# First MoE layer: products with packed values times w_in in place of x times w_in, parts of w_in kept in DRAM

## The chip, the cores and the metric

The kernel runs on one core of one Trainium2 chip. The metric is device time in microseconds (us) of one execution. The kernel before takes 1510.52 us, the median of three executions (1508.63 to 1512.57).

## The reference, cut to what matters

```python
# attention through 32 packs for each head: batch 8, heads 8, sequence 576, head_dim 64
p_packed = sm_attn(p, k, v)              # 32 packed rows of 64 for a head
out = sm_attn(q, p_packed, p_packed)     # softmax(q . p_packed) gives shares of 32 packs; shares @ p_packed
x = out.transpose(0, 2, 1, 3).reshape(4608, 512)
# first MoE: one dense hidden layer of 2048
h = x @ w_in                             # 512 -> 2048
g = h * clip(h + 3, 0, 6) / 6
x1 = g @ w_out                           # 2048 -> 512
# second MoE: 8 experts, one for each token, 512 -> 1024 -> 512
```

For one batch element, x is (shares of 8 heads x 32 packs = 256 numbers for each token) times a block matrix of packed values. So x @ w_in is also shares @ (packed values @ w_in), a product over 256 and not over 512, once the second factor is known.

## The kernel before

Every fp32 operand is split into an upper and a lower part of TensorE's faster format, and each product is made of three matmuls (`mm3`: upper by upper, upper by lower, lower by upper). PE is TensorE, DVE is VectorE, ACT is ScalarE, POOL is GpSimd, SP issues most DMAs.

The 4608 tokens go through the first MoE in 16 blocks of 288, two blocks to a batch element. A block has 16 steps (`g` counts steps over all blocks, `fc` in a block). A step has the first layer of 128 hidden units (`m1_l1`, PE tile `hps`, two halves), its activation (ACT `r`, then the gate on DVE, `m1_gate`), its split (ACT `gh`, POOL `gl`, `m1_split`), and the second layer of the step two before it (`m1_l2`, PE tiles `acc`). In PSUM there are two tiles `hps`, two tiles `tps` that everything else shares, and four `acc`.

Between the halves stand ticks, four to a step. Each tick lets every running generator do its next piece once its wait (a number of ticks in `WT`) is over: `qstage` turns the next block's q into x (scores `s2`, softmax over packs on DVE, then products `al` by `pbh` and `pbl`, which make x and its parts `xh`, `xl`), `kstage` makes the packed values of a batch element and one half of its heads (`pph`, `ppl` are their turned parts), and `m1_end` writes a finished block to DRAM and routes its tokens. One `kstage` runs in each of blocks 0 to 13. Each engine executes its instructions in the order in which they are written.

At the start the float64 weights w_in and w_out come in 32 pieces of 512 KB. `w_stage` turns each to fp32 parts in five stages over ACT, DVE and POOL. A hand-written string `ORDER` says which chain steps next, also inside block 0, up to the last weight piece. In the last block the first slots of the second MoE are chosen and loaded (`pre_slots`), and 12 slots of 384 tokens then run through the experts.

Of the kernel before, what the change touches and what calls it, by code (L numbers as in the profile page):

```python
# [36 lines left out]
WT = {  # L37
    "p": 4, "k": 4, "exp": 7, "aT": 6, "pp": 9, "ppT": 6, "q": 7, "s2": 6, "sm": 7, "out": 5, "w": 4, "x1": 8, "lp": 3,
    "oh": 6, "sc": 4, "s0": 0, "sw": 7, "ga": 0, "tu": 3, "y": 4, "tb": 1, "s1": 0, "s2q": 17, "y0": 9, "mp": 5,
}  # L40
# [4 lines left out]
ORDER = "dddeedeaddeeadbdebaadeaadaededaawaebeaeabfbbaabwbbbabbaffbafbwwafwfawwbwbabwagbabawawwbaaaggawgbwwwbwaabawbawwwggwwwwwbabwwwwwbwgwbwawwbaawwbwkwbwbwcawbwwbwwww.wwbbbkqwqwqww.qkwqww.qwwkwk.kqwkqwk.qqkwkqwqkw.kqk.wkwwwqwwqwkw.qqk.qkkqqwwwwqw..wqkkqwwwwqkqkwq.wwkw.qkwwwwqqww.qkwkqqwwwwqk...wkwwwkwqwqwkww.w.ww.qwqqwwww.wwwww..q.wwww.w....ww.wwww.ww.ww..w...w.ww..www..w.w.wwwwww....ww..www.w..w...wwww.ww..."  # L45
W_MIN = 2.0 ** -15  # the upper word of a float64 of 2**-127, read as a float32
# [3 lines left out]
def kernel(ctx, tc, q, k, v, p, w_in, w_out, mod_id, w_gate, mod_bias, w1, w2, out):  # L50
# [7 lines left out]
    # left: weights, constants, x of even blocks, attention; the last two make room for the second MoE  # L58
    # right: tiles of hidden layers, x of odd blocks, first the raw weights and then the first MoE's results
# [16 lines left out]
    tabd = dp.tile([NTAB, 2], I32, name="tabd")  # L76

# [28 lines left out]
    pph, ppl, pbh, pbl = [], [], [], []  # L106
    for hq in range(2):
        pph.append(ap.tile([128, 2, 128], F32R, name=f"pph{hq}"))
        ppl.append(ap.tile([128, 2, 128], F32R, name=f"ppl{hq}"))
        pbh.append(ap.tile([128, 2, 128], F32R, name=f"pbh{hq}"))  # L110
        pbl.append(ap.tile([128, 128], F32R, name=f"pbl{hq}"))
# [19 lines left out]
    def late_consts():  # L131
        # what only the start needs lies where weights will lie
# [27 lines left out]
        # token of column tg*32+i of a block, on partition (tg%3, i)  # L160
# [12 lines left out]
        # entries that no token fills: no output row, a row of zeros, no gate  # L173
# [33 lines left out]
    script = []  # L207

    def tick():
        if script:  # L210
            if scripted():
                return
            streams[:0] = [s for s in script if not s.done]
            script.clear()
# [13 lines left out]
    class Feed:  # L228
        """Half sequences of four heads of q or k, in order: their rows, turned and split by halves of d."""

        def __init__(self, src, units, depth, pool=None):
            self.apart = True  # runs as a chain of its own, at the start
            self.src, self.units, self.depth, self.pool = src, units, depth, pool
            self.raw, self.n, self.ready = [], 0, []
# [14 lines left out]
        def ahead(self):  # L249
            """[(h, c), (sg, si)] of the next half of d, which is 32e + c."""  # L250
# [38 lines left out]
    # the first heads go in two chains at once; the second one's tiles lie where weights will lie  # L289
# [25 lines left out]
    def turned(hi, lo, src, f=None):  # L315
        """[(h, n), (h % 2, e, c)], zeros elsewhere, to blocks of [(h, c), e, (h, n)] in two parts."""
# [16 lines left out]
    # rows of a pair of heads, the other rows, the pair  # L333
    pairs = [(slice(0, 64), slice(64, 128), 0), (slice(64, 128), slice(0, 64), 1)]

    def kstage(b, hq):
        """Scores of the packs, their weights, the packed values and their transposes."""
# [63 lines left out]
        while b > 0 and ("q", b - 1, 1, hq) not in done:  # L401
            yield 1
# [16 lines left out]
        for r, _, j in pairs:  # L419
            nc.scalar.copy(pbh[hq][r, j, :], mb[r])  # L420
        yield
        for r, o, j in pairs:
            nc.gpsimd.tensor_tensor(pbl[hq][r], mb[r], r32(pbh[hq][r, j, :]), op=ALU.subtract)
            nc.scalar.copy(pbh[hq][o, j, :], mb[r])
        yield from turned(pph[hq], ppl[hq], mb, mf)
# [5 lines left out]
    def qstage(b, hf, hq):  # L431
# [51 lines left out]
        for r, _, j in pairs:  # L483
# [8 lines left out]
            if j == 0:  # L492
                yield WT["out"]
# [643 lines left out]
```

## Time and profile before

| | us |
|---|---|
| median of three executions | 1510.5 |
| span of the profiled execution, first to last instruction | 1508.5 |
| start, to the first product of block 1 | 169.5 |
| blocks 1 to 13, each about | 61.0 |
| block 14 (no `kstage`) | 56.4 |
| block 15, to the first product of the second MoE | 65.9 |
| second MoE, to the end of the span | 423.0 |

The profiled execution's own time is its span and about 2 us around it, as the median lies 2.0 us above the span. Engines are asynchronous, so busy times overlap. A matmul's row lasts longer than its share of the time, since matmuls are pipelined: what one costs is read from start to start.

### The profile page before, as it was taken

The numbers are of one execution on the slowest core, as the hardware profiler recorded it, in microseconds if no ns is written. First come the engines' busy times: TensorE is split into PE (matmuls) and PEld (weight loads), VectorE is DVE, ScalarE is ACT, GpSimd is POOL, SyncE is SP. The second block draws the span as 40 slices with busy tenths as digits, with TensorE's granted clock in tenths as the row PEclk, the third lists the DMA queues.
The fourth block names the chain that finished last, engine by engine and source line by source line (L and its number), as shares of the span: only waits on it lengthen the run. The fifth ranks groups of instructions, "written<-read, shape, count | busy, mean of one in ns | idle before, by whom it ended". The sixth has DMA issues, their size and how long they took to land. (4 is left out here: it accounts for less than half of the span.)

```text
span 1508.5 us, 25124 instructions
## 1 busy us (share of the span) xinstructions
PE 1412.0 (94%) x9072; PEld 1329.4 (88%) x9072; DVE 898.4 (60%) x2211; ACT 684.7 (45%) x1503; POOL 673.4 (45%) x774
## 2 busy tenths in 40 slices
PE   3367899999999999999999999999999999999995
PEld 2257899999999999999999999999889999999994
DVE  8999756464465554645646556446666656566541
ACT  6556545454354454544544535433434434444430
POOL 3678644444444444444444444433135544444530
PEclk8578999999999999999999999999899999999998
DMA  9333112011120111111201110003336555555520
GB/s 273 126 135 100 42 25 59 23 49 40 26 66 24 41 47 29 55 42 25 64 18 48 40 33 33 17 1 118 102 121 209 168 172 165 172 168 194 180 89 30
DMA packets 111301, 127.03 MB, mean 84 GB/s; under 512 B 52163, under 2 KB 77892, under 8 KB 111172
## 3 DMA queue, kind: packets, MB, share of 16 engines
q1 hardware_dynamic: 102148, 106.41, 22.7%
q0 software_dynamic: 9024, 18.96, 3.7%
q8 instruction: 73, 1.20, 0.3%
q14 instruction: 56, 0.46, 0.1%
HBM read 105.80 MB, written 19.54 MB: 83 GB/s over the span
## 5 line engine op out<-in xcount | busy, mean ns | idle before, releaser
L97 POOL TENSOR_TENSOR gl<-r,gh 128x288 fp32r<-128x288 f32 x240 | 199.1, 830 | 277.0 <-ACT gh L96 212.2
L91 PE MATMUL acc<-gh,wh 128*128 128x288 f32 x1024 | 311.8, 304 | 2.3 <-ACT gh L96 1.2
L92 PE MATMUL acc<-gl,wh 128*128 128x288 f32 x1024 | 305.1, 298 | 8.1 <-POOL gl L97 6.0
L91 PE MATMUL hps<-xh,wh 128*128 128x288 f32 x1024 | 309.5, 302 | 1.7 <-issue 1.3
L93 PE MATMUL hps<-xh,wl 128*128 128x288 f32 x1024 | 306.5, 299 | 1.9 <-POOL wl L561 1.5
L92 PE MATMUL hps<-xl,wh 128*128 128x288 f32 x1024 | 305.6, 298 | 1.9 <-DVE xl L490 1.8
L93 PE MATMUL acc<-gh,wl 128*128 128x288 f32 x1024 | 306.3, 299 | 0.8 <-issue 0.8
L596 DVE SCALAR_TENSOR_TENSOR r<-r,hps 128x288 f32<-128x288 f32 x256 | 114.1, 446 | 226.6 <-ACT r L591 226.1
L794 POOL DMA_INDIRECT xg<-x1d,idx x144 | 152.7, 1060 | 171.3 <-DVE idx L789 131.1
L92 PEld LDWEIGHTS acc<-gl,wh 128*128 128x128 f32 x1024 | 195.0, 190 | 9.6 <-POOL gl L97 7.3
L91 PEld LDWEIGHTS acc<-gh,wh 128*128 128x128 f32 x1024 | 194.9, 190 | 8.3 <-ACT gh L96 1.8
L91 PEld LDWEIGHTS hps<-xh,wh 128*128 128x128 f32 x1024 | 196.4, 192 | 5.5 <-issue 1.1
L92 PEld LDWEIGHTS hps<-xl,wh 128*128 128x128 f32 x1024 | 196.5, 192 | 3.0 <-DVE xl L490 2.2
L93 PEld LDWEIGHTS hps<-xh,wl 128*128 128x128 f32 x1024 | 196.2, 192 | 2.6 <-POOL wl L561 1.8
L93 PEld LDWEIGHTS acc<-gh,wl 128*128 128x128 f32 x1024 | 194.9, 190 | 2.7 <-issue 2.7
L591 ACT ACTIVATE r<-hps,half 128x288 f32<-128x288 f32 x256 | 127.5, 498 | 131.0 <-PE hps L93 121.1
L274 POOL TENSOR_TENSOR hl<-tmp,hl 128x288 fp32r<-128x288 f32 x116 | 94.4, 824 | 149.1 <-ACT hl L271 149.0
L96 ACT CAST gh<-r 128x288 fp32r<-128x288 f32 x256 | 110.2, 430 | 67.8 <-DVE r L596 67.4
L97 DVE TENSOR_TENSOR wl<-wr,wh 128x1024 fp32r<-128x1024 f32 x96 | 114.6, 1222 | 32.7 <-ACT wh L96 15.9
L91 PE MATMUL hps<-x2h,wh 128*128 128x384 f32 x384 | 129.8, 338 | 0.9 <-DVE gl L841 0.9
L92 PE MATMUL hps<-x2l,wh 128*128 128x384 f32 x384 | 129.4, 337 | 0.4 <-issue 0.4
L93 PE MATMUL hps<-x2h,wl 128*128 128x384 f32 x384 | 129.7, 338 | 0.0
(260 smaller groups left out, 2622.1 us busy)
## 6 DMA issues: line engine op xcount, KB each, us to landing
wr<-in_moe_w_dram SPq DMA_DIRECT2D x96, 512.0 KB
raw<-in_k_dram SPq DMA_DIRECT2D x32, 288.0 KB
raw<-in_q_dram SPq DMA_DIRECT2D x32, 288.0 KB
x1d<-xo SPq DMA_DIRECT2D x16, 576.0 KB
wraw<-in_moe_w_in_dram SPq DMA_DIRECT2D x16, 512.0 KB
wraw<-in_moe_w_out_dram SPq DMA_DIRECT2D x16, 512.0 KB
v<-in_v_dram SPq DMA_DIRECT2D x64, 126.0 KB
xg<-x1d,idx POOLq DMA_INDIRECT x144
```

The costliest lines, as they stand in the source:

```text
L91: nc.tensor.matmul(o, lh, rh, start=start, stop=False)
L92: nc.tensor.matmul(o, lh, rl, start=False, stop=False)
L93: nc.tensor.matmul(o, ll, rh, start=False, stop=stop)
L96: nc.scalar.copy(hi, src)
L97: (eng or nc.vector).tensor_tensor(lo, src, r32(hi), op=ALU.subtract)
L274: eng.tensor_tensor(lo, f.rearrange("p s c -> p (s c)"), r32(hi), op=ALU.subtract)
L591: nc.scalar.activation(r, ph[:, :NB], AF.Relu, bias=half, scale=1.0 / 6.0)
L596: nc.vector.scalar_tensor_tensor(r, r, 1.0, ph[:, :NB], op0=ALU.min, op1=ALU.mult)
L794: nc.gpsimd.indirect_dma_start(out=self.xg[-1][:, o % 4, :], out_offset=None, in_=self.src, in_offset=bass.IndirectOffsetOnAxis(ap=self.id ...
```

## The change

The attention no longer makes x. `qstage` ends with the shares (turned, and split into `xh`, `xl` of two tiles in place of four), and `pbh`, `pbl`, `al` are gone. A new generator, `packs(b)`, multiplies the packed values of batch element b by all of w_in: 16 pieces of w_in (`wi`), 48 matmuls of 512 columns for a batch element, eight results `ppt`, each copied and split by ACT and DVE. `m1_l1` takes `ppt` as its weights and contracts over two tiles. So w_in itself is needed once for each batch element. There is no room to keep it: each piece's parts are written to DRAM at the start (`wind`) and read back (`wi_load`, six pieces ahead) for each later batch element, on SP's queue. `packs(b)` runs in the second block of the element before; its loads start at step 8 of the block before that. `kstage` moves one unit earlier (two in block 0, none in block 13). The part of `ORDER` that led block 0 is gone: block 0 forces the weights that its next steps need. A step has three ticks.

```diff
+    pph = [ap.tile([128, 2, 128], F32R, name=f"pph{i}") for i in range(4)]
-        while b > 0 and ("q", b - 1, 1, hq) not in done:
-            yield 1
-        for r, _, j in pairs:
-            nc.scalar.copy(pbh[hq][r, j, :], mb[r])
...
-        for r, _, j in pairs:
-            o = t_tile()
-            nc.tensor.matmul(o[:, :NB], pbh[hq][:, j, :], al[:, j, :], start=True, stop=False)
-            nc.tensor.matmul(o[:, :NB], pbl[hq][r], al[r, j, :], start=False, stop=True)
-            nc.scalar.copy(xh[:, 2 * hq + j, :], o[:, :NB])
-            nc.vector.tensor_tensor(xl[:, 2 * hq + j, :], o[:, :NB], r32(xh[:, 2 * hq + j, :]), op=ALU.subtract)
+        nc.scalar.copy(xh[:, hq, :], af)
+        yield
+        (nc.gpsimd if blk else nc.vector).tensor_tensor(xl[:, hq, :], af, r32(xh[:, hq, :]), op=ALU.subtract)
...
+        for u in k_units[:2] if w == 0 else k_units[w + 1:w + 2]:
+            yield from kstage(*u)
...
+                if kind == "i":
+                    nc.sync.dma_start(wind[u], r32(at[u]).rearrange("p a f -> p (a f)"))
...
+    def wi_load(u):
+        wi[u] = wp.tile([128, 2, 512], F32R, tag="w", name="wi")
+        nc.sync.dma_start(r32(wi[u]).rearrange("p a f -> p (a f)"), wind[u])
+
+    def packs(b):
+        at = [0]
+        def ahead(n):
+            while b and at[0] < min(16, n):
+                wi_load(at[0])
+                at[0] += 1
+        ahead(NWI)
+        while l1_at[0] < 32 * b - 16:
+            yield 1
+        for u in range(8):
+            j, hq = divmod(u, 2)
+            while b and l1_at[0] < 32 * b - 16 + 4 * max(0, j):
+                yield 1
+            ps = t_tile()
+            i = 2 * (b % 2) + hq
+            for e in range(2):
+                while b == 0 and w_done[0] < 8 * j + 2 * hq + e + 1:
+                    yield 1
+                w = wi.pop(2 * u + e)
+                mm3(ps, pph[i][:, e, :], ppl[i][:, e, :], w[:, 0, :], w[:, 1, :], start=(e == 0), stop=(e == 1))
+                del w
+                ahead(2 * u + e + 1 + NWI)
+                yield WT["x"] if e == 0 else None
+            t = ppt[b, u] = wp.tile([128, 2, 512], F32R, tag="w", name="ppt")
+            nc.scalar.copy(t[:, 0, :], ps)
+            yield
+            nc.vector.tensor_tensor(t[:, 1, :], ps, r32(t[:, 0, :]), op=ALU.subtract)
+            pk_done[0] = u + 1
+            del t, ps
+            yield WT["x"]
...
-        for kk in (0, 1) if part == 0 else (2, 3):
-            a = 256 * kk + 128 * (fc % 2)
-            mm3(ph[:, :NB], wh[:, a:a + 128], wl[:, a:a + 128], xh[:, kk, :], xl[:, kk, :],
-                start=(kk == 0), stop=(kk == 3))
+        for hq in range(2):
+            t = ppt[blk // 2, 2 * (fc // 4) + hq]
+            mm3(ph[:, :NB], t[:, 0, o:o + 128], t[:, 1, o:o + 128], xh[:, hq, :], xl[:, hq, :], start=(hq == 0), stop=(hq == 1))
...
-                    while w_done[0] < min(16, 2 * (fc // 2) + 2):
+                    while pk_done[0] < 2 * (fc // 4) + 2:
+                        (xstream if w_done[0] >= 8 * (fc // 4) + 4 else wstream).step()
+                    while fc >= 2 and w_done[0] < 8 * ((fc - 2) // 4) + 5 + (fc - 2) % 4:
                         wstream.step()
...
+                if fc == 8 and blk % 2 == 0 and blk // 2 + 1 < B:
+                    pstream = Stream(packs(blk // 2 + 1))
+                    pstream.step()
```

Three places show how the order moves. The first is DVE in block 0, behind the gate of the third step (`fc` 2) before and between the gates of the eighth and ninth (`fc` 7 and 8) now, with the conversion of weights (`t`, `wl`), the gates (`r`) and the split of packs (`ppt`). Before:

```order
L596 SCALAR_TENSOR_TENSOR r<-r,hps 128x288
L548 TENSOR_SCALAR t<-t 128x512
L549 TENSOR_SCALAR t<-t 128x512
L550 SCALAR_TENSOR_TENSOR t<-wraw,t 128x512
L561 TENSOR_TENSOR wl<-wraw,wh 128x512
L548 TENSOR_SCALAR t<-t 128x512
L549 TENSOR_SCALAR t<-t 128x512
L550 SCALAR_TENSOR_TENSOR t<-wraw,t 128x512
L490 TENSOR_TENSOR xl<-tps,xh 128x288
L377 TENSOR_REDUCE st<-a 128x1
```

Now:

```order
L530 TENSOR_TENSOR wi<-wraw,wi 128x512
L518 TENSOR_SCALAR t<-t 128x512
L519 TENSOR_SCALAR t<-t 128x512
L520 SCALAR_TENSOR_TENSOR t<-wraw,t 128x512
L518 TENSOR_SCALAR t<-t 128x512
L519 TENSOR_SCALAR t<-t 128x512
L520 SCALAR_TENSOR_TENSOR t<-wraw,t 128x512
L585 TENSOR_TENSOR ppt<-tps,ppt 128x512 x2
L437 STREAM_TRANSPOSE tmp<-tps 128x288
L441 TENSOR_REDUCE mx<-tmp 128x9
L442 TENSOR_TENSOR tmp<-tmp,mx 128x288
L607 SCALAR_TENSOR_TENSOR r<-r,hps 128x288
```

Before, one to three conversions stand between two of the first gates. Now six stand between the gate of step 7 and the two `ppt` (the rows show the last two), and the next four gates follow with one conversion or none between them.

The second place is PE where block 1 begins, at `kstage` (`hl` by `pth`, then the transposes by `ident` and the values `v`). Before:

```order
L91 MATMUL hps<-xh,wh 128x288
L92 MATMUL hps<-xl,wh 128x288
L93 MATMUL hps<-xh,wl 128x288
L91 MATMUL tps<-hl,pth 128x288
L92 MATMUL tps<-hl,pth 128x288
L93 MATMUL tps<-hl,ptl 128x288
L91 MATMUL hps<-xh,wh 128x288
```

Now:

```order
L93 MATMUL tps<-hl,pth 128x288
L94 MATMUL tps<-hl,pth 128x288
L95 MATMUL tps<-hl,ptl 128x288
L93 MATMUL tps<-hl,pth 128x288
L94 MATMUL tps<-hl,pth 128x288
L95 MATMUL tps<-hl,ptl 128x288
L379 MATMUL tps<-ident,a 126x128 x4
L380 MATMUL tps<-ident,a 72x128
L396 MATMUL tps<-v,a 128x256 x5
L93 MATMUL hps<-xh,ppt 128x288
```

The second `kstage` of block 0 does not fit into its ticks, and what is left of it stands in one piece ahead of block 1's first product.

The third place is PE in block 3, where `kstage`'s transposes take both tiles `tps`. Before:

```order
L91 MATMUL acc<-gh,wh 128x288
L92 MATMUL acc<-gl,wh 128x288
L93 MATMUL acc<-gh,wl 128x288
L389 MATMUL tps<-ident,a 126x128 x4
L390 MATMUL tps<-ident,a 72x128
L91 MATMUL hps<-xh,wh 128x288
```

Now:

```order
L95 MATMUL acc<-gh,wo 128x288
L93 MATMUL tps<-wi,pph_97 128x512
L94 MATMUL tps<-wi,pph_97 128x512
L95 MATMUL tps<-wi,ppl_101 128x512
L379 MATMUL tps<-ident,a 126x128 x4
L380 MATMUL tps<-ident,a 72x128
L93 MATMUL hps<-xh,ppt 128x288
```

The last product of a pack now ends right ahead of the transposes, and its tile is free for the second of them only after ACT's copy and DVE's subtraction.

## Rows read from the trace of the kernel before

**Rows 1.** The page's busy times: us, share of the span, instructions.

```profile
PE 1412.0 (94%) x9072; PEld 1329.4 (88%) x9072; DVE 898.4 (60%) x2211; ACT 684.7 (45%) x1503; POOL 673.4 (45%) x774
```

**Rows 2.** Stretches: length, busy by engine, granted clock, DMA share, GB/s.

```profile
core 0: us, PE busy (x) PEld busy (x) DVE busy (x) ACT busy (x) POOL busy (x), PEclk, DMA share, GB/s
0.00:63.00 63.00, 20.85 (x74) 15.07 (x74) 55.55 (x126) 37.77 (x81) 27.28 (x59) 0.73 0.67 201
63.00:169.50 106.50, 76.92 (x409) 69.03 (x409) 101.03 (x139) 62.41 (x128) 82.41 (x68) 0.81 0.31 106
...
597.30:658.30 61.00, 61.00 (x443) 59.05 (x443) 33.26 (x104) 28.34 (x72) 26.53 (x33) 1.00 0.14 40
963.20:1019.60 56.40, 56.40 (x416) 54.98 (x415) 26.70 (x82) 22.77 (x56) 22.62 (x29) 1.00 0.03 12
1019.60:1085.50 65.90, 60.15 (x419) 58.25 (x418) 39.06 (x109) 26.20 (x55) 15.81 (x19) 0.92 0.30 94
1125.00:1450.00 325.00, 325.00 (x1637) 294.05 (x1636) 194.52 (x318) 139.17 (x204) 158.19 (x150) 1.00 0.54 178
```

**Rows 3.** All that PE waited for from 169.5 to 1019.6 us.

```profile
PE tps L92 <- POOL hl L274: 0.3, 1, 0.3
PE acc L92 <- POOL gl L97: 0.2, 1, 0.2
```

**Rows 4.** PE's timeline in block 8, twelve matmuls from first to next: start, us.

```profile
597.26 0.29 PE L91 MATMUL hps<-xh,wh 128*128 128x288 f32 x1
...
598.86 0.29 PE L91 MATMUL acc<-gh,wh 128*128 128x288 f32 x1
```

**Rows 5.** PE's timeline at a pair of `al` products.

```profile
433.47 0.29 PE L485 MATMUL tps<-al,pbh 128*128 128x288 f32 x1
433.70 0.39 PE L486 MATMUL tps<-al,pbl 64*128 64x288 f32 x1
434.02 0.40 PE L91 MATMUL hps<-xh,wh 128*128 128x288 f32 x1
434.26 0.29 PE L92 MATMUL hps<-xl,wh 128*128 128x288 f32 x1
```

**Rows 6.** PE's timeline in the second MoE, three matmuls of 512 columns.

```profile
1214.80 0.40 PE L91 MATMUL acc<-wh,gh 128*128 128x512 f32 x1
...
1215.50 0.39 PE L91 MATMUL tps<-wh,gh 128*128 128x512 f32 x1
```

**Rows 7.** DVE's timeline in block 8, the gates of steps 6 and 7.

```profile
624.85 0.41 DVE L596 SCALAR_TENSOR_TENSOR r<-r,hps 128x288 f32<-128x288 f32 x1
...
632.45 0.46 DVE L596 SCALAR_TENSOR_TENSOR r<-r,hps 128x288 f32<-128x288 f32 x1
```

**Rows 8.** POOL's and PE's timelines: step 7's `gl`, and the matmul that first reads it.

```profile
635.22 0.81 POOL L97 TENSOR_TENSOR gl<-r,gh 128x288 fp32r<-128x288 f32 x1 [3.80 <-DVE rsm L694]
...
636.36 0.30 PE L92 MATMUL acc<-gl,wh 128*128 128x288 f32 x1
```

**Rows 9.** Groups of instructions over the whole span: count, busy us, mean ns, idle before.

```profile
L591 ACT ACTIVATE r<-hps,half 128x288 f32<-128x288 f32 x256 | 127.5, 498 | 131.0 <-PE hps L93 121.1 <-remote 5.1 <-POOL gl L97 4.3
L550 DVE SCALAR_TENSOR_TENSOR t<-wraw,t 128x512 int32<-128x512 int32 x32 | 31.0, 969 | 1.1
L561 POOL TENSOR_TENSOR wl<-wraw,wh 128x512 fp32r<-128x512 f32 x21 | 30.7, 1463 | 1.7 <-ACT wh L559 0.8 <-ACT t L545 0.7
L490 DVE TENSOR_TENSOR xl<-tps,xh 128x288 fp32r<-128x288 f32 x64 | 28.9, 452 | 68.8 <-ACT xh L488 68.8
L868 DVE TENSOR_SCALAR y<-acc,gate 128x512 f32<-128x512 f32 x12 | 9.0, 750 | 7.5 <-PE acc L93 6.4
L870 ACT ACTIVATE y<-acc,gate 128x512 f32<-128x512 f32 x12 | 8.3, 688 | 23.6 <-DVE gate L865 14.0 <-PE acc L93 3.7 <-PE tps L93 3.3
```

**Rows 10.** PE's timeline in block 15, two matmuls that waited for their issue.

```profile
1056.08 0.40 PE L91 MATMUL acc<-gh,wh 128*128 128x288 f32 x1 [1.02 <-issue]
1058.16 0.40 PE L92 MATMUL acc<-gl,wh 128*128 128x288 f32 x1 [1.69 <-issue]
```

More of the change, by code (lines that the diff above doesn't have):

```diff
@@ L105 @@
     ptl = ap.tile([128, 2, 128], F32R, name="ptl")
[L106 to L111, printed above, removed]
+    pph = [ap.tile([128, 2, 128], F32R, name=f"pph{i}") for i in range(4)]
+    ppl = [ap.tile([128, 2, 128], F32R, name=f"ppl{i}") for i in range(4)]
     tri = cp.tile([96, 96], BF16, name="tri")
@@ L400, in kstage @@
         yield WT["aT"]
[L401 to L402 removed]
+        assert b < 2 or ("q", b - 2, 1, hq) in done
         pp = s_tile()
@@ L418, in kstage @@
         del pp
-        for r, _, j in pairs:
-            nc.scalar.copy(pbh[hq][r, j, :], mb[r])
         yield
[L422 to L425, printed above, removed]
+        yield from turned(pph[2 * (b % 2) + hq], ppl[2 * (b % 2) + hq], mb, mf)
         yield WT["pp"]
@@ L501, in q_window @@
             yield from qstage(b, hf, hq)
+    k_units = [(b, hq) for b in range(1, B) for hq in range(2)]
     def k_window(w):
-        b, hq = w // 2 + 1, w % 2
-        if b < B:
-            yield from kstage(b, hq)
-    wt, wraw = [], []
+        for u in k_units[:2] if w == 0 else k_units[w + 1:w + 2]:
+            yield from kstage(*u)
+    wi, wo, wraw = {}, {}, []
+    pieces = []
+    for j in range(4):
+        pieces += [("i", 4 * j + u) for u in range(4)] + [("o", 4 * j + u) for u in range(4)]
     def w_load():
         n = len(wraw)
-        j, kind, part = n // 4, n // 2 % 2, n % 2
+        kind, u = pieces[n]
         if n < 30:
@@ L553, in w_stage @@
         else:
-            if n % 2 == 0 and s == 3:
-                wt.append((wp.tile([128, 1024], F32R, tag="w", name="wh"), wp.tile([128, 1024], F32R, tag="w", name="wl")))
-            o = slice(512 * (n % 2), 512 * (n % 2) + 512)
-            hi, lo = (t[:, o] for t in wt[n // 2])
+            kind, u = pieces[n]
+            at = wi if kind == "i" else wo
             if s == 3:
-                nc.scalar.copy(hi, lo_f)
-            else:
-                (nc.gpsimd if n % 3 else nc.vector).tensor_tensor(lo, lo_f, r32(hi), op=ALU.subtract)
+                at[u] = wp.tile([128, 2, 512], F32R, tag="w", name="w" + kind)
+                nc.scalar.copy(at[u][:, 0, :], lo_f)
+            else:
+                (nc.gpsimd if n % 3 else nc.vector).tensor_tensor(at[u][:, 1, :], lo_f, r32(at[u][:, 0, :]), op=ALU.subtract)
+                if kind == "i":
+                    nc.sync.dma_start(wind[u], r32(at[u]).rearrange("p a f -> p (a f)"))
                 wraw[n] = None
-                w_done[0] = (n + 1) // 2
+                w_done[0] = n + 1
     def w_stream():
@@ L575 @@
     w_done = [0]
+    ppt, l1_at, pk_done = {}, [0], [0]
+    def wi_load(u):
[31 more added lines that the diff above has]
+            yield WT["x"]
@@ L965, in start @@
             yield from qstage(0, 0, hq)
-        chains = {"a": start(0), "b": start(1), "d": fk.run(4), "e": fk2.run(4), "f": fq.run(2), "g": fq2.run(2), "w": ws}
-        order = iter(ORDER)
-        def scripted():
-            for x in order:
-                if x == ".":
-                    return True
-                if x == "c":
-                    late_consts()
-                elif x in chains:
-                    next(chains[x], None)
-            return False
-        scripted()
+        xs = packs(0)
+        chains = {"a": start(0), "b": start(1), "d": fk.run(4), "e": fk2.run(4), "f": fq.run(2), "g": fq2.run(2),
+                  "w": ws, "x": xs}
+        for x in ORDER:
+            if x == "c":
+                late_consts()
+            else:
+                next(chains[x], None)
         for x in "deabfg":
@@ L991 @@
                 if fc == 0:
-                    if script:
-                        streams[:0] = [s for s in script if not s.done]
-                        script.clear()
                     for s in at:
                         s.finish()
+                    if blk % 2 == 0 and blk:
+                        pstream.finish()
                     if blk < NBLK - 1:
```

93 lines of the change are left out of this document (33 added, 60 removed).

## The prediction

> **What bounds the kernel now.** I read the page's busy times first [rows 1]: PE is busy in 94% of the span, no other engine in more than 60%. An average does not say where that holds, so the next view is a table of stretches [rows 2]. Three kinds of stretch show. In blocks 1 to 13, the one of 61.00 us stands for all, PE is busy from first to last at a granted clock of 1.00, while DVE works 33 and ACT 28 us. The waits confirm it: from 169.5 to 1019.6 us PE waited 0.5 us in all [rows 3]. So there each PE microsecond removed shortens the span, until something else ends last. The start, to 169.5 us, is the opposite: DVE works 55.55 + 101.03 = 156.6 of 169.5 us, PE only 97.8, at a clock of 0.73 and 0.81. DVE sets the pace there, and PE work removed is worth nothing. Block 15 is mixed: 60.15 of 65.90 us, clock 0.92, and PE waits for its own issue [rows 10]. The second MoE is bound by PE and the change does not touch it.
>
> **What PE loses and gets in blocks 1 to 15.** Prices are read from start to start, since the rows themselves overlap.
>
> First layer: a step had 12 matmuls of 288 columns and now has 6, so a block loses 96. Twelve of them start within 598.86 − 597.26 = 1.60 us [rows 4], 0.133 each: 15 × 96 × 0.1333 = −192.0 us. Block 0's share I count as nothing, as DVE hides it.
>
> The products that made x: four pairs `al` by `pbh`, `pbl` in every window of a `qstage`. A pair takes 434.02 − 433.47 = 0.55 us, and the matmul behind it comes 0.24 later where 0.13 is usual [rows 5], together 0.66. Fourteen windows lie in blocks 1 to 14: 14 × 4 × 0.66 = −37.0 us.
>
> Packed values times w_in: 48 matmuls of 512 columns for each batch element, 1 to 7 in blocks 1, 3, ... 13. Three matmuls of that width start within 0.70 us in the second MoE [rows 6], 0.233 each: 7 × 48 × 0.233 = +78.4 us. The Trainium skill ("TensorE: Matmul & The Clock Gate", section "Back-to-back issue gap") says that in a real kernel matmuls of 512 columns follow each other every 131 ns or so, with weight loads hidden. By that the packs would cost an estimated 44 us and the sum would be 34 lower. The rows of this kernel disagree with it (0.233 at a clock of 1.00), and the measurement decides; I give that case no chance of its own.
>
> Every `kstage` runs one block earlier, so block 13 loses its own and block 0 gets a second one. Block 14, which has none, takes 56.4 us against 61.0 [rows 2]: −4.6 us.
>
> Sum for PE: −192.0 − 37.0 + 78.4 − 4.6 = −155.2 us. Everything below eats into it.
>
> **The start (+29 us, between 8 and 55).** DVE's work there grows: a second `kstage` costs it 33.26 − 26.70 = 6.6 us [rows 2]; eight splits of `ppt`, 512 columns out of PSUM, between the 0.452 of a 288-column split and the 0.750 of a 512-column operation from PSUM [rows 9], nearest to the second, 8 × 0.75 = 6.0; the old x needed ten operations of about 0.45 more than the new: −4.5. Together +8. That is the lower bound, if DVE stays as busy as it was.
>
> It will not, since the first layer of a group of four steps now needs two finished `ppt`. The order shows six conversions between two gates and then four gates nearly bare: PE gets its work in bursts. At three of these groups DVE must look on: last piece on POOL 1.46, three matmuls 0.70 or more, copy on ACT 0.69, split on DVE, six matmuls 0.80, activation 0.50 [rows 4, 6, 9]. Some DVE work fills that; I take 4 us each, +12. The rest of the second `kstage` stands in one piece ahead of block 1's first product. Such a unit is 4.6 us of PE, 6.6 of DVE and 28.34 − 22.77 = 5.6 of ACT [rows 2]; wholly in a row that is 17, partly overlapped some 12, of which 6.6 is counted: +5. The packs of batch element 0 are 48 × 0.233 = 11 us of PE at full clock and 15 at the 0.75 granted there: +4. The upper bound is 8 us for each of three chains, the `kstage` in a row (+10) and those 15 us of packs nearly exposed (+13): 55.
>
> **New stalls in blocks 1 to 14 (+31 us, between 9 and 62).** PE waits for nothing there only because its queue is longer than every chain. The tightest place I found is step 7 of a block. In block 8 its gate starts 7.6 us after that of step 6 [rows 7], where a step is 61.0/16 = 3.8, as DVE is taken up by other generators' work. POOL's `gl` of that step ends at 635.22 + 0.81 = 636.03 and PE reads it at 636.36 [rows 8]: 0.33 us of slack. The change takes six matmuls out of each of the two steps between, 12 or 1.6 us, and leaves DVE's chain as it is: a stall of 1.3. What is late then is PE itself, and all steps behind it. Without stalls a block with no packs becomes 61.0 − 12.8 − 2.6 = 45.6 us, against some 33 of DVE and with a tick fewer per step to spread it: I take 2 us each for seven. A block with packs becomes 56.7, gives some slack back, and I take 1 us for its gates. But packs bring a new wait: the two tiles `tps` serve everything, and transposes that follow a pack wait for ACT's copy and DVE's split, 0.69 + 0.75 with what is queued on both, less the first transposes that cover it: 1 to 1.5, one place per block or two. I take 1.5. 7 × 2 + 7 × 2.5 = 31. Below, one stall of 1.3 per block without packs: 9. Above, twice what I take: 62.
>
> The rest of the change lies beside this. ACT's copies of `ppt` (0.69 each, eight in a block) replace copies of x that are gone. The parts of w_in are written in the start, 16 transfers of 512 KB on SP's queue, and read back seven times, 58.7 MB; the DMA share is 0.14 in a block now [rows 2], so I cost them at nothing (price in the last rival). **Block 15** has fewer ticks for the weight splits of the second MoE: some three, of 1.2 us or so, are left over, +2 (0 to 8).
>
> **Sum.** 1508.5 − 155.2 + 29 + 31 + 2 = 1415 for the span. The execution takes 2.0 us more than its span, and it lies at the median of the runs shown: 1417 us.
>
> **The rivals.**
>
> *Hidden after all.* Stalls and start reach only their lower bounds: 1508.5 − 155.2 + 8 + 9 + 2.0 = 1372. For it: POOL and ACT are half idle [rows 1], and DVE has 12 us of room even in the shorter block. Against it: the slack of 0.33 [rows 8] is smaller than the 1.6 taken away.
>
> *Chains decide.* Start and stalls reach their upper bounds: 1508.5 − 155.2 + 55 + 62 + 2 + 2.0 = 1474. For it: where PE waits, its clock does not stay at 1.00 (0.73 and 0.81 in the start, 0.92 in block 15 [rows 2]), and a block whose PE idles would pay for its matmuls twice. Against it: 94% busy leaves it far from there; block 15 idles 9% and still has 0.92.
>
> *The read-back starves the packs, slower than before.* A pair of blocks has to bring 16 pieces of 512 KB. SP takes its list in order; a load waits until PE is done with a buffer, and the loads of q, k and v stand behind it. Loads start at step 8 of the even block, so 16 pieces have some 23 + 57 = 80 us, 5 us each, 105 GB/s. In the second MoE the same queues move 178 GB/s at a share of 0.54 [rows 2], which speaks against it. The packs' gain is gone, with the 31 of stalls and 29 of start, when a pair of blocks takes its old 122 us less the 4 or so that those two cost; with the loads spread over 118 − 23 = 95 us that is 6 us a piece, 88 GB/s, half of what is shown. At 7 us a piece seven pairs take 7 × 16 more than that: some 1620.
>
> That the change does not do what it says I can exclude: the order shows six first-layer matmuls a step.
>
> **How the numbers follow.** The sum with its own range, 1396 to 1440: 0.55. Hidden after all, below 1396: 0.22. Chains decide, 1440 to 1505: 0.18. Starved: 0.05, of which 0.02 ends within 0.3% of the time before, which is about what a measurement of this kernel can tell from no change. The range 1378 to 1460 leaves out the lowest two fifths of the second case (0.09) and some 0.11 of the last two. Faster 0.95, same 0.02, slower 0.03.
>
> **What would show it.** Matmuls of packs 0.233 us from start to start, right; 0.13, and the sum is 34 too high. Block 1's first product at 198 us (178 if the start hides all, 225 if nothing). Blocks without packs 48 us, with packs 59; PE waiting there on POOL's `gl` or DVE's gate at steps near 7, and on `tps` at transposes. PE waits that end with a DMA of `wi` would mean the last rival; a granted clock below 1.00 in blocks 2 to 14, the third. Block 15 at 53 to 56 us. I am wrong above all if stalls sum up from step to step instead of being caught up: one us more in each step of 14 blocks would be 220.

## The result, and the profile after

The changed kernel takes 1525.8 us (median of four executions, 1522.4 to 1526.9) against 1511.1 for the kernel before: a ratio of 1.0092 with a 95% interval of 1.0077 to 1.0108. It is slower by 0.9%, where 1417 us, 1378 to 1460, was forecast. The profiled execution took 1526.6 us, its span 1524.8.

The page's busy times and the stretches that answer to [rows 1, 2]; columns as there.

```profile
PE 1304.8 (86%) x7792; PEld 1190.2 (78%) x7792; DVE 894.8 (59%) x2209; ACT 656.9 (43%) x1407; POOL 631.2 (41%) x716
```

```profile
0.00:83.50 83.50, 23.42 (x78) 16.86 (x78) 49.31 (x119) 31.45 (x66) 23.55 (x57) 0.68 0.56 172
83.50:235.10 151.60, 86.11 (x373) 68.11 (x373) 103.40 (x158) 71.25 (x140) 82.38 (x70) 0.66 0.45 152
644.50:699.20 54.70, 50.24 (x346) 47.72 (x344) 31.75 (x98) 23.96 (x62) 23.64 (x29) 0.97 0.37 122
699.20:760.60 61.40, 56.85 (x381) 52.69 (x380) 37.34 (x108) 28.82 (x71) 23.70 (x29) 1.00 0.32 108
931.20:988.60 57.40, 54.44 (x353) 51.38 (x353) 30.07 (x87) 24.25 (x58) 20.48 (x25) 0.94 0.27 95
988.60:1038.60 50.00, 45.07 (x313) 43.92 (x312) 24.69 (x78) 20.03 (x50) 21.25 (x27) 0.93 0.04 13
1038.60:1094.50 55.90, 48.93 (x324) 46.98 (x324) 35.13 (x107) 23.59 (x52) 16.39 (x18) 0.91 0.33 101
```

Stage by stage, in us:

| | before | after | forecast |
|---|---|---|---|
| start, to the first product of block 1 | 169.5 | 235.1 | 198 |
| blocks 1 to 14 | 850.1 | 803.5 | 739 |
| block 15 | 65.9 | 55.9 | 53 to 56 |
| second MoE, to the end of the span | 423.0 | 430.3 | 423, and +2 at the handover |

So PE's work did go away (107 us of busy time), and three places gave more than that back: the start, the waits in the blocks, and the handover to the second MoE. In the start DVE does the work it did before, 152.7 us, but in 235 us. In the blocks, which had no waits [rows 3], PE now waits. This is all that it waited for from 235.1 to 1038.6 us (us in total, times, longest; the list without its last row, 0.7 us).

```profile
PE acc L94 <- POOL gl L99: 14.1, 26, 0.9
PE tps L665 <- ACT a L365: 9.8, 6, 1.6
PE tps L665 <- ACT x1h L660: 9.3, 9, 1.3
PE tps L380 <- DVE ppt L585: 5.8, 6, 1.0
PE tps L94 <- POOL hl L266: 5.5, 12, 0.5
PE tps L666 <- DVE x1l L662: 4.6, 10, 0.6
PE acc L93 <- ACT gh L98: 3.7, 2, 2.2
PE tps L93 <- ACT hl L263: 3.6, 6, 0.6
PE acc L93 <- ACT x1f L639: 3.2, 6, 0.6
PE tps L380 <- DVE x1f L671: 3.0, 6, 0.5
```

In the table of stretches the same time is this row.

```profile
235.10:1038.60 803.50, 739.98 (x4997) 694.47 (x4996) 470.06 (x1393) 360.50 (x900) 325.88 (x400) 0.98 0.32 106
```

No row of the waits ends with a transfer. Waits for the gates' parts (`gl`, `gh`) are 17.8 of 63 us; most stand at products of the attention and the router. The router's two products (L665, L666) have the most, 23.7 us. One of their waits, in block 8, seen on three engines: PE at the router's first product, ACT ahead of it, DVE ahead of that (start, us, engine, line; in brackets the idle time before, and its releaser).

```profile
661.98 0.29 PE L95 MATMUL tps<-hl,ptl 128*128 128x288 f32 x1
663.54 0.32 PE L665 MATMUL tps<-x1h,wg 128*32 128x288 f32 x1 [1.26 <-ACT x1h L660]
664.38 0.32 PE L666 MATMUL tps<-x1l,wg 128*32 128x288 f32 x1 [0.52 <-DVE x1l L662]
...
665.84 0.45 PE L94 MATMUL hps<-xl,ppt 128*128 128x288 f32 x1
666.08 0.45 PE L95 MATMUL hps<-xh,ppt 128*128 128x288 f32 x1
```

```profile
659.27 0.42 ACT L263 CAST hl<-tmp 128x288 fp32r<-128x288 f32 x1
661.95 0.43 ACT L455 CAST xh<-tmp 128x288 fp32r<-128x288 f32 x1 [2.25 <-DVE tmp L452]
662.31 0.85 ACT L263 CAST hl<-tmp 128x288 fp32r<-128x288 f32 x2
663.06 0.43 ACT L660 CAST x1h<-x1f 128x288 fp32r<-128x288 f32 x1
663.39 0.43 ACT L98 CAST gh<-r 128x288 fp32r<-128x288 f32 x1
```

```profile
659.78 0.45 DVE L447 TENSOR_REDUCE sm<-tmp 128x9 f32<-128x288 f32 x1
...
661.44 0.48 DVE L452 STREAM_TRANSPOSE tmp<-tmp 128x288 f32<-128x288 f32 x1
```

ACT has nothing else to do than to wait for the end of the shares' softmax on DVE (2.25 us), and `x1h`, which does not depend on it, stands behind `xh` in its queue. PE stands for `x1h`. Right after, PE's matmuls start 0.24 us apart and not 0.13 [rows 4]: the lower of the clock's two levels. The block's granted clock is 0.97 where it was 1.00.

Two prices of the prediction have their rows here: three matmuls of a pack start 0.23 us apart, as taken.

```profile
734.71 0.39 PE L93 MATMUL tps<-wi,pph 128*128 128x512 f32 x1
734.94 0.39 PE L94 MATMUL tps<-wi,pph 128*128 128x512 f32 x1
735.17 0.40 PE L95 MATMUL tps<-wi,ppl 128*128 128x512 f32 x1
```

From starts of all matmuls in blocks 8 and 9, each at its own usual distance, PE's work is 46.7 and 55.1 us. It was forecast as 45.6 (with one pack less in it) and 56.7. The rest of 54.7 and 61.4 us, 8.0 and 6.3, is stall; 2 and 2.5 had been taken. Stall in this sense is more than idle time: it also holds what matmuls lose by starting further apart than usual, behind a wait or at the lower clock.

### The profile page after: what moved, and what is told of

It is laid out like the page before. It is cut to its first block, busy times and chain, and to the rows that moved or that the text cites. A ratio compares the mean times of both kernels' runs of the same rounds, so it can differ in the third digit from the quotient of the medians.

```text
span 1524.8 us, 22700 instructions
## 1 busy us (share of the span) xinstructions
PE 1304.8 (86%) x7792; PEld 1190.2 (78%) x7792; DVE 894.8 (59%) x2209; ACT 656.9 (43%) x1407; POOL 631.2 (41%) x716
## 5 line engine op out<-in xcount | busy, mean ns | idle before, releaser
L94 PE MATMUL acc<-gl,wo 128*128 128x288 f32 x1024 | 312.6, 305 | 16.2 <-POOL gl L99 15.7
L93 PE MATMUL acc<-gh,wo 128*128 128x288 f32 x1024 | 311.9, 305 | 14.0 <-ACT gh L98 7.9
L99 POOL TENSOR_TENSOR gl<-r,gh 128x288 fp32r<-128x288 f32 x240 | 194.3, 810 | 298.3 <-ACT gh L98 285.6
L95 PE MATMUL acc<-gh,wo 128*128 128x288 f32 x1024 | 309.9, 303 | 2.9 <-POOL wo L530 2.9
L807 POOL DMA_INDIRECT xg<-x1d,idx x144 | 152.7, 1061 | 162.6 <-DVE idx L802 122.3
L94 PEld LDWEIGHTS acc<-gl,wo 128*128 128x128 f32 x1024 | 199.0, 194 | 26.7 <-POOL gl L99 21.7
L93 PEld LDWEIGHTS acc<-gh,wo 128*128 128x128 f32 x1024 | 198.5, 194 | 23.7 <-ACT gh L98 11.6
L95 PEld LDWEIGHTS acc<-gh,wo 128*128 128x128 f32 x1024 | 199.4, 195 | 3.7 <-POOL wo L530 3.5
L93 PE MATMUL hps<-xh,ppt 128*128 128x288 f32 x512 | 159.5, 311 | 35.5 <-ACT ppt L583 27.9
L95 PE MATMUL hps<-xh,ppt 128*128 128x288 f32 x512 | 155.7, 304 | 0.6 <-issue 0.4
L94 PE MATMUL hps<-xl,ppt 128*128 128x288 f32 x512 | 155.1, 303 | 0.0
L93 PEld LDWEIGHTS hps<-xh,ppt 128*128 128x128 f32 x512 | 100.7, 197 | 39.6 <-ACT ppt L583 30.1
L98 ACT CAST wh<-wr 128x1024 fp32r<-128x1024 f32 x96 | 96.9, 1049 | 20.7 <-DMA wr<-in_moe_w_dram 20.7
L854 DVE SCALAR_TENSOR_TENSOR gl<-hps,gh 128x384 fp32r<-128x384 f32 x92 | 51.0, 554 | 90.4 <-ACT gh L853 68.7
```

The lines of the kernel that those rows point to most:

```text
L93: nc.tensor.matmul(o, lh, rh, start=start, stop=False)
L94: nc.tensor.matmul(o, lh, rl, start=False, stop=False)
L95: nc.tensor.matmul(o, ll, rh, start=False, stop=stop)
L98: nc.scalar.copy(hi, src)
L99: (eng or nc.vector).tensor_tensor(lo, src, r32(hi), op=ALU.subtract)
L807: nc.gpsimd.indirect_dma_start(out=self.xg[-1][:, o % 4, :], out_offset=None, in_=self.src, in_offset=bass.IndirectOffsetOnAxis(ap=self.id ...
```

## The experiments

Kernels of one group ran on one chip, each beside the kernel before, and ratios are to that (the changed kernel's is 1.0092). Numbers 1 to 4 met 1511.7 us for the kernel before, 5 to 8 another chip's 1497.6, 9 to 11 1510.6, 12 1515.7 (one execution), 13 and 14 1511.7. What one stage does is read from the one profiled execution of each.

### 1. Ticks between lumps of the shares

A lump is a run of one generator's instructions on an engine, with no tick in it, for whose end another engine waits.

```diff
@@ qstage, behind the subtraction of mx
-        yield
+        yield 1
...
@@ qstage, behind the transposition to aT
-        yield
+        yield 2
```

> The changed kernel with one tick between the DVE work of the scores' softmax and ACT's exponential that waits for it, and two ticks between the transposed shares and ACT's copy into xh; the work is the same. Theory A (in blocks 1 to 14 ACT stands 2 to 3 us in its queue for a lump on DVE, and behind it stand the router's x1h and the gates' gh, for which PE waits): the wait of 1.4 to 1.8 us at the router's first product and those of 0.6 to 1.2 us at gl near step 10 shrink, blocks of 54.7 and 61.4 us come to 51 to 53 and 58 to 60, 25 to 50 us less in all, near 1485. Theory B (PE has become too short between a step's first and second layer for any order of the same chains): the stalls only move, blocks within 0.7 us of what they are, 1515 to 1535. Theory C (transfers of parts of w_in disturb): no change either.

Measured: 0.9993 (0.9973 to 1.0013), 1510.2 us. Blocks 2 to 12 came to 631 us together, from 633; nearly all of the gain lies in block 13 (57.4 to 51.2) and block 14 (50.0 to 41.6), where no `kstage` runs. In block 8 the wait at the router's product went and another came some three us later at the same line of the router, 2.4 us, where `x1h` stood behind ACT's exponential of `kstage`. In blocks 2 to 12 theory A, with these lumps at fault, fails, and the stalls move, as B says. In blocks 13 and 14 A holds: PE is busy all but 0.2 us of each, at a clock of 1.00 in place of 0.94 and 0.93. The time of 1510.2 lies between the two forecasts.

```profile
926.60:977.80 51.20, 51.01 (x353) 48.69 (x352) 31.14 (x87) 24.41 (x58) 20.73 (x25) 1.00 0.30 106
977.80:1019.40 41.60, 41.38 (x313) 40.90 (x312) 26.30 (x77) 19.98 (x50) 20.95 (x26) 1.00 0.04 16
```

### 2. Without the read-back

```diff
-            while b and at[0] < min(16, n):
+            while b and at[0] < min(1, n):
...
-                w = wi.pop(2 * u + e)
+                w = wi[0] if b else wi.pop(2 * u + e)
```

> The changed kernel, but for batch elements 1 to 7 only one of the 16 pieces of w_in is read back and stands in for all of them, so 15 of 16 reads (55 MB) are left out and the packs of those elements have other values; matmuls and their order are the same. Theory C (the read-back costs: contention in DMA, or loads of q, k and v held up on SP's queue): blocks 2 to 12 become shorter, by 2 us each or more, 1490 to 1505. Theories A and B: no wait of PE in these blocks ends with a transfer, so blocks stay within 0.5 us and the time within 1519 to 1530.

Measured: 1.0065 (1.0047 to 1.0083), 1520.6 us. Blocks 2 to 12 are what they were, 53.9 to 54.7 and 61.4. Theory C is out for the blocks; the 5 us less lie in the start (232.2) and in the second MoE.

### 3. Without the packs of batch elements 1 to 7

```diff
-            t = ppt[blk // 2, 2 * (fc // 4) + hq]
+            t = ppt[0, 2 * (fc // 4) + hq]
...
...
-                if fc == 8 and blk % 2 == 0 and blk // 2 + 1 < B:
-                    pstream = Stream(packs(blk // 2 + 1))
-                    pstream.step()
```

> The changed kernel, but packed values times w_in are worked out for batch element 0 alone and used for all (48 matmuls, eight copies and splits and 16 reads less in each of seven blocks; the output of elements 1 to 7 is not the reference's). By 48 x 0.232 an odd block loses 11.1 us: 61.4 becomes 50.3 if nothing else comes or goes, as it does by theory A, 78 us in all, near 1447. If the tiles tps that packs hold cost the 1 to 1.5 us that the prediction took, odd blocks come to 49. If packs also cover stalls (PE has work while gates are late), odd blocks come to the length of even ones, 53 to 55, and only 45 to 60 us are gained.

Measured: 1458.9 us in one execution. Blocks 8 and 9 in its table of stretches:

```profile
602.90:655.40 52.50, 47.64 (x339) 45.01 (x338) 31.99 (x100) 24.14 (x63) 23.64 (x29) 1.00 0.17 48
655.40:708.70 53.30, 48.84 (x340) 46.64 (x339) 32.06 (x100) 24.34 (x63) 23.58 (x29) 0.97 0.16 46
```

Odd blocks lose 8 us and not 11: they end at the length of even ones. With some 45 us of work in it a block still takes 52 to 53. So the chains of a block with a `kstage` and a `qstage` allow no less as they stand, and a part of the packs' 11 us had been free.

### 4. Constants early

The five loads of `late_consts` (modality ids, `w_gate`, bias) move into `const_loads`.

```diff
-        early_consts()
+        const_loads()
+        early_consts()
```

> The changed kernel with the five loads of router constants (modality ids, gate weights, bias) issued right after the first loads on SP and not at 66 us behind the loads of weights; the operations that use them stay where they are. In the changed kernel DVE waits 11.6 us and ACT 13.0 us for them, from 70 to 82.7 us, and the copy and split of the first ppt stand behind that. If this wait sets the first product of block 0 (83.5 us), it comes 10 to 13 us earlier, and so does block 1 (235 to 222 to 226): 1511 to 1516. If the weights of the next steps are late anyway, block 0 starts earlier but block 1 moves less than 4 us: 1521 to 1527.

Measured: 1.0001 (0.9986 to 1.0016), 1511.2 us; the first product of block 0 at 70.5 in place of 83.5, block 1 at 223.2 in place of 235.1. The wait did set this part of the start. In the changed kernel it is this row of DVE's waits from 60 to 90 us, and SP's timeline tells why the load came so late: SP stood 8 us at loads of weights.

```profile
DVE scr L182 <- DMA scr<-in_moe_modality_id_dram: 11.6, 1, 11.6
```

```profile
58.39 7.89 SPq L496 DMA_DIRECT2D wraw<-in_moe_w_out_dram  x2
66.37 7.26 SPq L149 DMA_DIRECT2D scr<-in_moe_modality_id_dram  x3
```

### 5. Each first-layer product twice

```diff
-        for hq in range(2):
+        for hq in (0, 1, 0, 1):
             t = ppt[blk // 2, 2 * (fc // 4) + hq]
```

> The changed kernel, but each step's six first-layer matmuls are written twice (the second time they overwrite the first; the result is the same). PE's nominal work in a block grows by 96 x 0.133 = 12.8 us, back to about what a block had in first-layer products before the change. Theory B (a stall is a chain on ACT, DVE and POOL that PE's queue no longer covers): the added work fills the stalls. Blocks of 54.7 and 61.4 us grow only to their nominal work, 59.7 to 60.7 and 68.0 to 69.0, by 5 to 7 us each and not by 12.8. Theory D (each transfer of data between engines costs PE a fixed time, however long its queue): blocks grow by 12 to 13 us, to 67 and 74.

Blocks 8 and 9 in the table of stretches of this kernel (1639.7 us in one execution):

```profile
708.30:769.40 61.10, 60.10 (x440) 58.76 (x440) 31.65 (x98) 24.35 (x62) 23.73 (x29) 1.00 0.34 110
769.40:839.40 70.00, 68.25 (x476) 65.30 (x475) 37.41 (x108) 29.32 (x71) 23.74 (x29) 1.00 0.28 95
```

12.8 us of matmuls more made these blocks 6.5 and 8.6 us longer. Stalls fell from 8.0 and 6.3 to 1.7 and 2.1 us, with DVE, ACT and POOL doing what they did. Nothing but PE's own work changed, so most of the stalls are chains that this work had covered. Both blocks end about 1 us or less above theory B's ranges and 4 to 6 us below D's values: B holds, D does not. A step has three ticks here too, so having fewer ticks than before (four) can alone account for no more than the 2 us that are left. It is also the place of the wrong step: 2 and 2.5 us of stall is right for a block with the old amount of work.

### 6. More ticks between lumps

Experiment 1's edit and

```diff
-    "p": 4, "k": 4, ... "lp": 3,
+    "p": 4, "k": 5, ... "lp": 4,
...
@@ kstage, ahead of the exponential
-        yield
+        yield 2
```

> The changed kernel with ticks between lumps: as in the first experiment (one tick ahead of the exponential of the shares, two ahead of ACT's copy to xh), and two ahead of the exponential of kstage, a wait of 5 for 4 in kstage's products and 4 for 3 at the router's products. Theory A (a few lumps at fixed places hold up ACT's queue): with the next one also moved, blocks come to 51 to 53 and 58 to 60 us, 1475 to 1495 in all. Theory B (PE's queue too short for these chains wherever they stand): a stall at one place gives way to another, blocks 53 to 55 and 60.5 to 62, and the time stays within 10 us of the 1510 of the first experiment.

Measured: 0.9866 (0.9849 to 0.9882), 1478.0 us. Blocks are 51.2 and 58.7, as A had it, so the order of the chains does matter once several lumps are moved together. Blocks 1 to 14 take 45 us less than in the changed kernel; the start took 7 us more (block 1 at 242.3). The granted clock in its blocks 1 to 14 is 1.00 (0.98 in the changed kernel), so a part of the 45 us is the clock:

```profile
242.30:1000.50 758.20, 726.13 (x4996) 683.69 (x4995) 468.58 (x1392) 360.72 (x900) 323.81 (x398) 1.00 0.35 113
```

### 7. Second layer three steps behind

```diff
...
-            if g >= 2:
+            if g >= 3:
                 for part in range(2):
-                    m1_l2(g - 2, part)
+                    m1_l2(g - 3, part)
```

> The changed kernel with the second layer three steps behind the first and not two (four buffers for gh and gl). It takes away waits of PE for gl and gh alone: in block 8 1.16 + 0.36 us, in block 9 0.63 + 0.72. By theory B, if gates are what is late, blocks 2 to 13 lose 1.3 to 2 us each, and PE, further ahead, comes no earlier to the attention's products: 15 to 28 us in all, 1498 to 1511. If the stalls at attention and router products then take up what is gained, less than 8 us: 1518 to 1526.

Measured: 1.0165 (1.0139 to 1.0191), 1520.8 us on the chip where the kernel before took 1497.6, so worse than the changed kernel and than either forecast. PE's waits for `gl` and `gh` went; blocks 2 to 12 became 56.1 to 56.7 and 61.5 to 63.1 us. PE's first waits in blocks 8 and 9 are now

```profile
PE tps L665 <- ACT x1h L660: 4.6, 2, 2.9
PE tps L94 <- POOL hl L266: 1.4, 3, 0.5
```

Gates were not what PE lacked. Moving PE ahead brought it earlier to products that were not ready: in blocks 1 to 14 the router's products waited 29.9 us (23.7 in the changed kernel), and waits for DVE's gate at the first layer (3.8) and for `ppt` at the values of `kstage` (5.9) are new.

### 8. A conversion at every tick in block 0

```diff
-    "w": 4,
+    "w": 0,
```

> The changed kernel with a piece of weights converted at every tick in block 0 (wait 0 for 4), so that the three runs of five to six conversions ahead of steps 4, 8 and 12 become short. In these runs a piece took 3.5 us (ACT waits for POOL's addition at each), while PE and the gates stood. If the runs set the start, block 1 begins 15 to 35 us earlier than at 235, at 200 to 220, and the time is 1490 to 1511. If DVE's work sets it (153 us busy before 235), or the conversions push the second kstage to the block's end, block 1 begins within 8 us of 235.

Measured: 1.0070 (1.0048 to 1.0092), 1507.6 us; block 1 at 228.3, 7 us earlier. The long runs are gone (at most five conversions stand between two steps), yet from block 0's first product to that of step 12 it takes 117.1 us, in the changed kernel 119.4. Spread out, the conversions take about as long.

### 9. All waits halved in block 0

```diff
-                self.wait = next(w for w in self.gen if w is not None)
+                self.wait = next(w for w in self.gen if w is not None) // (2 if l1_at[0] < 16 else 1)
```

> The changed kernel with every wait of a running generator halved in block 0 alone (work, loads and their order on SP as before in kind). Both kstages then end in step 12 of block 0 and nothing of them is left in one piece ahead of block 1's first product; conversions of weights and packs spread over the steps. In the changed kernel DVE is idle for some 80 of the first 235 us, 13 of them for router constants. Theory E (order: pieces that run alone, at the end and ahead of steps 4, 8 and 12, set the start): block 1 begins at 200 to 215 us, 1490 to 1507 on a chip where the changed kernel has 1525. Theory F (the packs' own chain, conversion to product to split to first layer, sets it wherever the rest stands): block 1 begins at 225 to 237, 1515 to 1528.

Measured: 1.0045 (1.0024 to 1.0066), 1518.3 us; block 1 at 229.9. Alone, this gives 5 us: theory E fails here. But the edit did only half of what was meant. The piece ahead of block 1 shrank: from the first product of step 15, the last, to block 1 it takes 4.8 us, in the changed kernel 22.7. Six conversions still stand ahead of steps 8 and of 12, and step 12 begins at 213.7 in place of 202.9.

### 10 and 11. Edits together

Experiment 6 with `"p": 6`, experiment 4, and experiment 9's line; in 11 with `// (3 if ...`.

> Four edits together: the spread of the sixth experiment (with a wait of 6 for 4 at the start of kstage), constants loaded early, waits halved in block 0. If the causes found add up: start 235 less 12 for the constants and 15 to 30 for the order, 193 to 208; blocks 51 and 58.7 as in the sixth, less up to 1 us each at kstage's first products; end as there. Some 35 to 50 us below the sixth's 1478 on the same chip, a ratio of 0.955 to 0.965 to the kernel before. If the start is set by the packs' chain, 0.975 to 0.98.

> The same as the one before, with waits in block 0 cut to a third: no run of conversions is left ahead of step 12, and the loads of weights come earlier in SP's order. Theory E: block 1 begins another 3 to 10 us earlier than with half. If DVE's work (153 us before block 1) is reached, or loads are late, within 3 us of it.

Measured: 0.9570 (0.9554 to 0.9586), 1445.5 us, block 1 at 213.5; and 0.9513 (0.9497 to 0.9528), 1437.7 us, block 1 at 206.7. Blocks are 49.8 and 58.4 in both. With constants early (223.2), shorter waits in block 0, with the spread, bring 10 and then 7 us more. Experiment 10's ratio is as forecast, its start is not (193 to 208 was); in 11 the gain of 7 us is as theory E has it.

### 12. Block 0 without its packs

```diff
     def packs(b):
+        if b == 0:
+            for u in range(8):
+                ppt[b, u] = wp.tile([128, 2, 512], F32R, tag="w", name="ppt")
+                nc.gpsimd.memset(r32(ppt[b, u]), 0.01)
+                pk_done[0] = u + 1
+            return
...
```

> The eleventh experiment's kernel (constants early, spread, waits in block 0 cut to a third), but batch element 0's packs are not worked out: its ppt are filled with a constant, 48 matmuls, eight copies and eight splits are left out of the start, and the first layer of block 0 waits for no piece of w_in (the output of element 0 is not the reference's). All pieces of both weights are still converted and written. There block 1 began at 206.7 us. Theory F (what is left of the start is the packs' own chain in front of the first layer, product, copy, split, with the clock at half speed): block 1 begins at 165 to 182 us. Theory G (conversion of 32 pieces over ACT, DVE and POOL, and SP's queue, set it): within 12 us of 206.7, less 8 us for the splits and copies, 190 to 207.

Block 1 began at 208.5 us, against 206.7 in the eleventh: theory F is out, and G's range ends just below. (Constants in place of element 0's packs route tokens otherwise and lengthen the second MoE by 73 us, so the kernel's time, 1516.0 in one execution, says nothing.) DVE was busy 103.6 of the 120 us from 60 to 180. That points to conversions as what sets the pace there, though DVE was less full than in the kernel before (84.2 of the 87 us from 63 to 150). What they lacked seems to be time ahead of that: in the eleventh DVE worked 48 of the first 70 us, where before it worked 55.6 of 63 [rows 2].

### 13 and 14. Pieces of w_in in four transfers

That pointed at the first loads. From 12 to 16 us the table of stretches has these rows for the kernel before, the changed kernel, and experiment 13, in this order (the last two numbers are the DMA engines' share and GB/s).

```profile
12.00:16.00 4.00, 2.08 (x15) 1.80 (x15) 3.28 (x11) 3.39 (x9) 0.00 (x0) 1.00 1.06 373
```

```profile
12.00:16.00 4.00, 2.71 (x13) 1.80 (x11) 1.03 (x4) 2.48 (x5) 0.00 (x0) 1.00 0.26 105
```

```profile
12.00:16.00 4.00, 2.92 (x18) 2.19 (x17) 3.82 (x12) 3.60 (x8) 0.00 (x1) 1.00 1.06 243
```

The edit, in 13 alone and in 14 on top of the eleventh:

```diff
-            src = bass.AP(src.tensor, src.offset, [[64 * 2 * FF, 4], [2 * FF, 32], [1, 1024]])
+            for h in range(4):
+                nc.sync.dma_start(t.rearrange("p f w -> p (f w)")[32 * h:32 * h + 32],
+                                  bass.AP(src.tensor, src.offset + 64 * 2 * FF * h, [[2 * FF, 32], [1, 1024]]))
...
```

> The changed kernel, but each of the 16 pieces of w_in from the input comes in four transfers of 32 rows in place of one of 4 x 32 rows; bytes, places and all else are the same. In the changed kernel DMA engines are busy 0.25 to 0.32 while such a piece comes alone (97 to 114 GB/s, some 5 us a piece, 80 us for 16), where the kernel before has 0.8 to 1.0 and 220 to 370 GB/s. Theory H (the pattern of this load uses a quarter of the DMA engines, and all loads behind it in the start wait, v, constants, the next weights): share near 1 in the first 25 us, the first product of block 0 at 63 to 75 in place of 83.5, block 1 10 to 25 us earlier, 1500 to 1515. If the same rows are slow in any grouping, or SP's issue of 64 transfers takes as long: within 4 us of the changed kernel.

> The eleventh experiment's kernel (spread, constants early, waits in block 0 cut to a third) with the same four transfers for a piece. Theory H: DVE's idle time of some 22 us in the first 70 us shrinks to 8 to 12 and the conversions after it never wait for a piece; the first product of block 0 at 55 to 62 (70.0), block 1 at 188 to 198 (206.7), some 9 to 18 us below the eleventh on the same chip, a ratio of 0.940 to 0.946. If conversions (DVE 52 of 60 us busy from 60 to 180) set it alone: only the 8 to 12 us of the first part are gained, or less than 4 if constants early had already taken them.

Measured: 0.9907 (0.9885 to 0.9930), 1498.0 us; the first product of block 0 at 56.6 in place of 83.5, block 1 at 207.4 in place of 235.1, blocks as in the changed kernel. Theory H holds, and the gain is somewhat larger than its ranges. This one edit turns the change from slower to faster. And 0.9445 (0.9429 to 0.9460), 1427.2 us, for 14: block 1 at 194.8, 5.6% below the kernel before, all as forecast. Its blocks 1 to 14 in one row, and PE's two largest waits there:

```profile
194.80:940.20 745.40, 718.29 (x4995) 684.09 (x4994) 469.72 (x1386) 362.49 (x899) 325.10 (x398) 1.00 0.36 114
```

```profile
PE hps L93 <- DVE r L614: 6.8, 7, 1.0
PE tps L672 <- ACT a L370: 6.0, 6, 1.0
```

## Why the prediction was wrong, by its own steps

The forecast for the span was 1415 and the span is 1524.8: 110 us, of which 37 lie in the start, 65 in blocks 1 to 14, and 8 behind them.

**PE's terms held.** First-layer products at 0.133, packs at 0.23, `al` pairs and the moved `kstage` give blocks of 46.7 and 55.1 us of work, 101.8 together, where 102.3 was forecast. The 131 ns for 512 columns that the Trainium skill states ("TensorE: Matmul & The Clock Gate", section "Back-to-back issue gap") are not met here either.

**The start (+29 taken, +65.6 measured).** A term was missing: the change also writes w_in's load anew, 4 groups of 32 rows in place of two groups of 128, which neither the section on the change nor the sum names. Each of these loads moves at a share of 0.26, 105 GB/s, and SP's later loads queue behind it. Taken away (experiment 13) the start is 27.7 us shorter, and what is left, +37.9, lies within the 8 to 55 given. The Trainium skill ("DMA: Bandwidth & Descriptors", section "Why a DMA increments its semaphore by 16 and not by 1") says that a transfer is split over the largest number of engines, up to 16, that divides the slowest dimension of both sides. By that the source's 4 groups and the tile's 128 rows give 4 engines of 16; the share of 0.26 agrees, and so does the return to 1.06 with slowest dimensions of 32. Within the 37.9, DVE's work did not grow by 8 us (152.7 against 156.6), and the packs' chain ahead of the first layer, 12 us of the sum, costs nothing that can be seen in experiment 12 (on the eleventh's kernel). Constants (12 us, experiment 4) are not a further term on top of the load: SP came to them late because it stood at weights, and in experiment 13 DVE waits for no constant up to 90 us. The piece of `kstage` ahead of block 1, +5 in the sum, was taken too small: from the first product of step 15 to block 1 it takes 22.7 us (22.6 in experiment 13), before 4.2, and 3.8 in 11 and 14. The 16.5 us between experiments 4 and 11 (223.2 to 206.7) all come from this end; from block 0's first product to step 15 it takes 129.1 and 132.9. How the rest divides between order, a clock of 0.64 to 0.66, and conversions is not settled.

**Stalls (+31 taken, 62 as the upper bound, 95.8 measured).** This is the step that failed by its size: 803.5 us less the 707.7 of forecast work (850.1 − 155.2 + 12.8 of block 15). PE's idle time is 63.5 us of it (803.50 − 739.98); in the rest matmuls started further apart than usual. I priced the tightest gate, 0.33 us of slack [rows 8], and set the upper bound as twice my own value, which is no bound from rows. Slack at one place told nothing of the others. Every chain from DVE through ACT to PE, of the attention and the router as of the gates, had been covered by the same 12.8 us of work in a block that the change takes away. Experiment 5 shows it for blocks 8 and 9: with that work put back, stalls are at the 2 us that I took. Experiments 1 and 7 show that one repair only moves the stalls in blocks 2 to 12, and 6 and 14 that the order of these chains is what can be mended: blocks 1 to 14 at 745.4 us have stalls of 38, near the 31. The lower clock level is a part of it: a mean of 0.98 over 803.5 us costs an estimated 12 to 20 us (0.015 to 0.025 of it), if PE is busy while it lasts.

**The wait of transposes for a pack's tile** was right: six waits of 1.0 us for `ppt` in 803 us (1.5 taken), one in each odd block that has both.

**Block 15 and the second MoE (−10.8 taken, −2.7 measured).** Block 15 gained 10.0. The second MoE, whose instructions did not change, took 7.3 more, all of it in its first 70 us (its 300th matmul starts that much later after its first). From its first product to its last it took 413.0 us, before 405.8, and in the experiments, the twelfth aside, 404.5 to 416.4. It may depend on how the handover falls; the cause is open.

**The rivals.** The read-back, the one on the slower side, is not what made it slower (experiment 2). "Chains decide" named the mechanism, with a chance of 0.18 and a price of 1474 that was too small. What I held against it, that 94% busy leaves the clock far from falling, did not hold: blocks 8, 13 and 14 have 0.97, 0.94 and 0.93.

## What to carry to other kernels

When a change takes work from the engine that is busy all the time, ask what that work covered: list each chain that feeds the engine in a step, not only the tightest, and price the case in which none is covered. An upper bound is made from such a list, not from a multiple of one's estimate. Read every rewritten load as a change of its own, its access pattern too: here an unremarked line cost 28 us and the sign of the result.

## What the runs showed of the hardware that was not expected

- A load of 512 KB whose source is 4 groups of 32 rows moved at 105 GB/s and a DMA share of 0.26. With four loads of 32 rows for each piece the same stretch has a share of 1.06.
- After PE had stood for some 2.4 us (661.98 to 664.54, two matmuls in it) its matmuls started 0.24 us apart in place of 0.13, though it was busy all the while. In kernels with less stall (experiments 6 and 14) the mean granted clock of blocks 1 to 14 is 1.00.
- The same kernel, the one before, took 1497.6 us on one chip and 1510.6 to 1511.7 on others (1515.7 in one execution on a further one).
